# Projections with a queue for each half of the array, 28 more staged groups of maxima, and attention steps of two or three maxima, in a transformer block on one core

## The chip, the core and the metric

One NeuronCore of a Trainium2 chip runs the whole block as one program. The metric is the device time of one execution in microseconds; "time before" is the median of three runs. The engines are TensorE (PE; its weight loads are listed as PEld), VectorE (DVE), ScalarE (ACT), GpSimd (POOL) and SyncE (SP), which here only issues DMAs. TensorE writes to PSUM, which has eight banks of 512 float32 columns on each of 128 partitions.

## The reference

All inputs are float32: x is 2048 x 640, wqkv 640 x 1920, wo 640 x 640, w_gate and w_up 640 x 1728, w_down 1728 x 640. There are 32 heads of 20.

```
q, k, v = split_heads(layernorm(x) @ wqkv)          # 32 heads of 20
p = softmax(q @ k.T * 20 ** -0.5)                   # exact, over 2048 keys
h = x + merge_heads(p @ v) @ wo
out = h + (silu(layernorm(h) @ w_gate) * (layernorm(h) @ w_up)) @ w_down
```

## The kernel before

The program has three stages: the projections to q, k and v, the attention, and the output projection with the feed-forward part. Matmuls whose precision matters are done as three products of values split into a high part and a low part.

**Units and groups.** The 32 heads lie in 8 groups g of 4, and the 2,048 queries in 4 chunks c of 512, which makes 32 attention units u = 4g + c. A head has 20 rows; two heads with the two parts of each make stacks of 60 rows, so that one stack lies in the upper half of the array's rows (partitions 0 to 63, b = 0) and another in the lower half (64 to 127, b = 1). Matmuls in different halves run side by side.

**Maxima.** The softmax needs the largest score of every query before its unit starts. For a unit u, a chunk kc of keys, a tile t of 128 queries and two pairs of heads in both halves there are four products of 128 x 512 scores. They are taken in one of two ways. In attention, `max_one` (products at L274, maxima at L280) does one product of 512 columns into a PSUM bank (`ps_max`, 3 banks there) and one VectorE maximum over it, so that such a set costs four products and four maxima. In the projections, `max_four` does a *staged group*: with keys stored as differences between the two halves of a chunk, four products of 256 columns write a - b to two banks, ScalarE takes the ReLU of each (L251), four products add b (all eight at L239), since max(a, b) = relu(a - b) + b, and VectorE takes a maximum over each bank (L261). `in_projections` says which sets are staged: all of u = 0, and for units with c = 0 or 1 (and u = 2) key chunks 0 and 1. That is 144 groups. The other 1,472 products wait in the lists `singles[0]` and `singles[1]`, one for each half, in the order of the units.

**Projections.** Token chunks c = 0 to 3 are projected one after another: ten blocks of 128 rows of q and k (`query_key`, 512 columns a product) and eight blocks of values (`value`, 320 columns a product), each as 15 products in `rounds` (L643). A product over 128 rows is cut into two of 64 rows. Both halves of a block add to the same PSUM bank, so the second halves must come after the first: `behind` holds them, `second_half` issues one when 20 are waiting, and an instruction on VectorE that does nothing (L648) tells TensorE that the first halves are done. Three banks take blocks, five take maxima. After each product `visit` looks whether something else may be issued: a staged group's second products, a step of the layer norm of the next chunk, a `flip` (transposes of normalised tokens, L569), or a new group. It decides by a planner's clock per engine (`clock`, `takes`) with a duration for each kind of instruction; `held` says when banks come free. Blocks go out through ScalarE copies, GpSimd subtractions (L90) and DMAs to DRAM (L615); staged groups load keys and queries back from DRAM in *items* (L176 on SP's queue), up to six at a time. The order that comes out is fixed in the program.

**Attention.** A unit has 16 steps kt of 128 keys; there are 512 steps. A step follows a string such as `"WsSmmSsM"`: s and S are a score product of 128 x 512 in the upper or lower half (L1303, bank `ps_one`, four in turn) with its exponential on ScalarE (L1309), m and M a maximum from `singles[0]` or `singles[1]`, and W weighs the values of the step two back (L1313; four products, listed as eight). Two strings alternate, with two m and one M or the other way. When the lists are empty, steps have no maximum. Weights of the later stage are prepared on GpSimd meanwhile. The copy of a finished unit is at L1323.

Of the kernel before, what the change touches and what calls it, by code (L numbers as in the profile page):

```python
# [14 lines left out]
ALU = mybir.AluOpType  # L15
# [25 lines left out]
ORDER = ("WsSmmSsM", "WSsMMsSm")  # L41


@with_exitstack
def tile_block(ctx: ExitStack, tc: tile.TileContext, x, wqkv, wo, wg, wu, wd, out):
# [168 lines left out]
    def max_pair(mx, q, k, pair, t, kc, k0):  # L214

        banks = [ps_max() for _ in range(2)]
        for b, ps in enumerate(banks):
            rows = slice(b * ROW, b * ROW + NPART)
            nc.tensor.matmul(
                ps, q[rows, pair, t * P : (t + 1) * P], k[rows, pair, k0 : k0 + CH],  # L220
                start=True, stop=True,
            )
        done = takes("PE", 240)
        for b, ps in enumerate(banks):
            nc.vector.tensor_reduce(
                mx[:, b, pair, t, kc : kc + 1], ps, axis=AX.X, op=ALU.max
            )
            hold([takes("DVE", 600, done + 205) + 100])

    def max_four(mx, q, k, t, kc):  # L230

        banks = [ps_max() for _ in range(2)]
        half = CH // 2

        def products(cols, first):
            for pair in range(2):
                for b in range(2):
                    rows = slice(b * ROW, b * ROW + NPART)
                    nc.tensor.matmul(  # L239
                        banks[b][:, pair * half : (pair + 1) * half],  # L240
                        q[rows, pair, t * P : (t + 1) * P], k[rows, pair, cols],
                        start=first and pair == 0, stop=True, skip_group_check=True,
                    )

        until = [[1e9] for _ in banks]

        def differences():
            products(slice(half, CH), True)
            done = takes("PE", 240)
            for ps in banks:  # L250
                nc.scalar.activation(ps, ps, AF.Relu)  # L251
                takes("ACT", 478, done + 150)
            hold(*until)
            return clock["ACT"] + RELU

        def maxima():
            products(slice(0, half), False)
            done = takes("PE", 240)
            for b, ps in enumerate(banks):
# [3 lines left out]
                    axis=AX.X, op=ALU.max,  # L263
                )

        return differences, maxima

    def max_one(u, kc, t, pair, b):

# [1755 lines left out]
```

## Time and profile before

| | |
|---|---|
| median of 3 runs | 2015.58 us (2015.23 to 2016.2) |
| the profiled execution | 2017.19 us, of which its span 2015.4 |
| first projection product in halves (L643) | 20.9 us after the span's start |
| first score (L1303), last score | 317.9, 1452.7 us |
| busy in the span | PE 2002.7, PEld 1247.8, DVE 1603.9, ACT 1437.1, POOL 796.8 us |
| granted TensorE clock | 1.00 |

A line of a group in the profile reads: source line, engine, operation, output <- input with partitions x elements, count | busy us, mean ns of one | idle time of the engine before, and who ended it. A line of the timeline reads: start, duration, engine, source line, operation, count. A line of a table by stage gives, after the length of the stage, each engine's busy time and the number of its instructions. TensorE's matmuls are pipelined: each is listed with about 0.4 us, but the next of the same half starts 0.12 to 0.23 us later, so starts are compared and not durations.

### The profile page before, as it was taken

To read this page: it belongs to the slowest core of one execution; us is meant where nothing else is said; L and a number is where in the kernel's file an instruction comes from. 1 tells how busy PE (TensorE), PEld (TensorE's weight loads), DVE (VectorE), ACT (ScalarE), POOL (GpSimd) and SP (SyncE) were. 2 spreads that over 40 slices of the span, in tenths; PEclk is the share of its full clock that TensorE was granted. 3 is DMA by queue.
4 is the path that set the end of the run, shared out by engine and by line. 5 is a ranking of instruction groups with operands and counts; after the bars stand their busy time and mean duration, and the time that the engine had idled before them with its cause. 6 is when DMAs were issued, how large, how long until landed. Compare 5 with 4: busy or idle time off the path is not lost.

```text
span 2015.4 us, 40030 instructions
## 1 busy us (share of the span) xinstructions
PE 2002.7 (99%) x14354; PEld 1247.8 (62%) x14354; DVE 1603.9 (80%) x2806; ACT 1437.1 (71%) x2819; POOL 796.8 (40%) x1190
## 2 busy tenths in 40 slices
PE   9999999999999999999999999999999999999999
PEld 8999995333333333333333333345598888888888
DVE  5677778888888888888888988886387666676677
ACT  4678878999999999999999999986633222212221
POOL 7465423333443443343400011011156444754555
PEclk9999999999999999999999999999999999999999
DMA  7777563352634544535513022321159654974642
GB/s 252 255 251 264 179 204 86 117 150 92 190 104 135 159 128 133 160 122 164 172 40 88 22 75 71 94 63 56 40 185 312 223 187 154 354 274 156 206 150 94
DMA packets 199340, 310.35 MB, mean 154 GB/s; under 512 B 53744, under 2 KB 87856, under 8 KB 198120
## 3 DMA queue, kind: packets, MB, share of 16 engines
q1 hardware_dynamic: 192552, 284.21, 43.8%
q0 software_dynamic: 6496, 23.60, 3.9%
q8 instruction: 114, 1.87, 0.4%
q14 instruction: 82, 0.67, 0.1%
q10 hardware_dynamic: 96, 0.00, 0.0%
HBM read 208.11 MB, written 99.19 MB: 152 GB/s over the span
## 4 chain that ended last, share of the span: by engine, by line
PE 96%; DMA 1%; DVE 1%; POOL 1%; issue 0%; ACT 0%; SPq 0%; POOLq 0%; DVEq 0%; ACTq 0%
PE acc L1313 24%; PE ps_a L1481 17%; PE ps_one L1303 15%; PE ps_max L274 12%; PE ps_one L643 10%; PE ps_b L1576 9%; PE ps_max L239 3%; PE ps_max L1031 2%; PE ps_b L1031 2%; PE ps_two L805 0%; PE ps_two L696 0%; DVE mx L261 0%; DMA rb<-r_d 0%; DVE mx L280 0%; PE ps_max L1066 0%
## 5 line engine op out<-in xcount | busy, mean ns | idle before, releaser
L1309 ACT ACTIVATE probs<-ps_one 128x512 f32<-128x512 f32 x2048 | 1056.1, 612 | 61.9 <-PE ps_one L1303 35.0
L280 DVE TENSOR_REDUCE mx<-ps_max 128x1 f32<-128x512 f32 x1472 | 924.5, 683 | 107.0 <-PE ps_one L1303 73.2
L1303 PE MATMUL ps_one<-q_stk,k_stk 62*128 62x512 f32 x2048 | 580.6, 449 | 1.0 <-DMA q_stk<-m_d 1.0
L1313 PE MATMUL acc<-probs,v_stk 128*32 128x512 f32 x4096 | 546.3, 605 | 0.1
L1303 PEld LDWEIGHTS ps_one<-q_stk,k_stk 62*128 62x128 f32 x2048 | 248.0, 184 | 436.6 <-ACT probs L1309 413.9
L274 PE MATMUL ps_max<-k_stk,q_stk 60*128 60x512 f32 x1472 | 374.9, 426 | 1.1 <-DVE mx L261 0.9
L274 PEld LDWEIGHTS ps_max<-k_stk,q_stk 60*128 60x128 f32 x1472 | 272.5, 186 | 29.7 <-DVE mx L280 2.8
L1698 DVE TENSOR_TENSOR tmp<-ps_a,tmp 128x512 f32<-128x512 f32 x208 | 141.2, 689 | 121.0 <-PE ps_a L1481 94.0
L261 DVE TENSOR_REDUCE mx<-ps_max 128x2 f32<-128x512 f32 x288 | 180.6, 684 | 63.8 <-PE ps_max L239 60.2
L1313 PEld LDWEIGHTS acc<-probs,v_stk 128*32 128x32 f32 x4096 | 80.9, 108 | 179.8 <-issue 167.9
L251 ACT ACTIVATE ps_max<-ps_max 128x512 f32<-128x512 f32 x288 | 151.6, 583 | 42.8 <-PE ps_max L239 40.2
L1576 PE MATMUL ps_b<-halves,yp 128*128 128x320 f32 x1032 | 178.7, 308 | 0.2 <-DVE h L1581 0.2
L1576 PEld LDWEIGHTS ps_b<-halves,yp 128*128 128x128 f32 x1032 | 165.2, 188 | 16.0 <-DVE h L1581 0.5
L1481 PE MATMUL ps_a<-t,units 128*128 128x512 f32 x624 | 162.5, 396 | 0.0
L90 POOL TENSOR_TENSOR yp<-y,yp 128x256 fp32r<-128x256 f32 x96 | 60.4, 630 | 186.9 <-ACT yp L89 186.9
L1481 PE MATMUL ps_a<-z,units 128*128 128x512 f32 x516 | 133.9, 394 | 0.0
L1481 PEld LDWEIGHTS ps_a<-t,units 128*128 128x128 f32 x624 | 112.6, 188 | 18.5
L1348 POOL TENSOR_TENSOR o<-o,rb 128x512 f32<-128x512 f32 x31 | 39.9, 1286 | 199.8 <-DMA q_stk<-m_d 72.7
L1581 DVE TENSOR_TENSOR h<-ps_b,h 128x320 f32<-128x320 f32 x248 | 109.7, 480 | 5.8 <-PE ps_b L1576 4.3
L643 PE MATMUL ps_one<-z_hi,w_lo 64*128 64x512 f32 x380 | 113.3, 392 | 0.0
L643 PE MATMUL ps_one<-z_lo,w_hi 64*128 64x512 f32 x380 | 112.1, 392 | 0.0
L643 PE MATMUL ps_one<-z_hi,w_hi 64*128 64x512 f32 x380 | 111.5, 393 | 0.0
(224 smaller groups left out, 2651.7 us busy)
## 6 DMA issues: line engine op xcount, KB each, us to landing
units<-w_d SPq DMA_DIRECT2D x186, 256.0 KB
w_d<-stage SPq DMA_DIRECT2D x106, 256.0 KB
halves<-j_d SPq DMA_DIRECT2D x70, 320.0 KB
j_d<-stage SPq DMA_DIRECT2D x42, 320.0 KB
k_stk<-k_d SPq DMA_DIRECT2D x64, 160.0 KB
q_stk<-q_d SPq DMA_DIRECT2D x64, 160.0 KB
raw<-k_d SPq DMA_DIRECT2D x62, 160.0 KB
raw<-q_d SPq DMA_DIRECT2D x54, 160.0 KB
```

The lines of the kernel that those rows point to most:

```text
L251: nc.scalar.activation(ps, ps, AF.Relu)
L261: nc.vector.tensor_reduce(mx[:, b, :, t, kc], ps.rearrange("p (j n) -> p j n", j=2), axis=AX.X, op=ALU.max,)
L274: nc.tensor.matmul(ps, queries[u][rows, pair, t * P : (t + 1) * P], keys[u // NC][rows, pair, kc * CH : (kc + 1) * CH], start=True, stop=True,
L280: nc.vector.tensor_reduce(mxs[u][:, b, pair, t, kc : kc + 1], ps, axis=AX.X, op=ALU.max)
L643: nc.tensor.matmul(ps, a[rows], b[rows], start=(i == n == 0), stop=(i == 1 and n == last), skip_group_check=True,)
L1303: nc.tensor.matmul(ps, keys[u // NC][rows, p, kt * P : (kt + 1) * P], queries[u][rows, p, :], start=True, stop=True,)
L1309: nc.scalar.activation(probs[p][:, b, :], ps, AF.Exp, scale=scale)
L1313: nc.tensor.matmul(acc[32 * j : 32 * j + 32, :], values[u // NC][:, kt, j * VW : j * VW + 32], probs[j // 2][:, j % 2, :], start=(kt == 0) ...
L1481: nc.tensor.matmul(ps.rearrange("p (t n) -> p t n", t=TPC), w[k][:, i], z[k][:, :, j], start=(first and m == 0), stop=(last and m == len(n ...
L1576: nc.tensor.matmul(ps, a, b, start=(n == 0), stop=(n == len(pairs) - 1))
L1581: nc.vector.tensor_tensor(out=h, in0=ps, in1=h, op=ALU.add)
L1698: add = lambda out, ps, x: nc.vector.tensor_tensor(out=out, in0=ps, in1=x, op=ALU.add)
```

## The change

It has four parts.

1. *A queue for each half.* The planner keeps a time for each half of the array (`lane`), and `other_work` fills whichever is behind. `max_half` takes the place of `max_four`: a staged group becomes two half groups, each with one bank, whose four products are issued one at a time. Second halves of blocks are issued when the planner's time for their first halves has passed, with no fixed lag of 20. The instruction that tells of this (L691 now) goes to VectorE, ScalarE or GpSimd, whichever clock is least, and is issued later, when the first halves should be done. A new half group also waits until VectorE's clock is at most 1,200 ns ahead. A `flip` waits until the layer norm's steps are done.
2. *28 more staged groups*: key chunk 2 of the units u = 4, 8, ... 28. Differences of chunk 2 of the keys are therefore stored for all blocks, and 14 more items are loaded. 172 groups are staged in all, and 1,360 products are left for attention.
3. *Attention:* from step 48 on every fourth step (kt = 3, 7, 11, 15) follows `"WsSmMsS"`, with two maxima.
4. *The end of the maxima of unit 0* uses VectorE's transpose and DMAs (`max_parts`, `max_turn`, `max_load`, as other units do) in the place of a transpose on TensorE (`max_finish`).

```diff
+SHORT = "WsSmMsS"
+FULL_STEPS = 3 * NT
...
-    def max_four(mx, q, k, t, kc):
+    def max_half(mx, q, k, t, kc, b):
+        half, until, own = CH // 2, [1e9], []
+        rows = slice(b * ROW, b * ROW + NPART)
+        def product(pair, cols, first):
             nc.tensor.matmul(
+                own[0][:, pair * half : (pair + 1) * half],
+                q[rows, pair, t * P : (t + 1) * P], k[rows, pair, cols],
+                start=first and pair == 0, stop=True, skip_group_check=True,
             )
+            return spend(b, 118)
+        def difference(pair):
+            if pair == 0:
+                own.append(ps_max())
+                hold(until)
+            done = product(pair, slice(half, CH), True)
+            if pair == 1:
+                nc.scalar.activation(own[0], own[0], AF.Relu)
+                return takes("ACT", 478, done + 150) + RELU
+        def maximum(pair):
+            done = product(pair, slice(0, half), False)
+            if pair == 1:
+                until[0] = takes("DVE", 600, done + 205) + 100
                 nc.vector.tensor_reduce(
+                    mx[:, b, :, t, kc], own[0].rearrange("p (j n) -> p j n", j=2),
                     axis=AX.X, op=ALU.max,
                 )
...
-        return u == 0 or (kc < 2 and (u % NC < 2 or u == 2))
+        return u == 0 or kc < 2 and (u % NC < 2 or u == 2) or kc == 2 and u % NC == 0
...
+    def maxima(b, new=True):
+        if pending[b]:
+            pending[b].pop(0)()
+            return True
+        pe = max(clock["PE"], lane[b])
+        if seconds[b] and seconds[b][0][0] <= pe + SLACK:
+            f = seconds[b].pop(0)[1]
+            f(0)
+            pending[b].append(lambda: f(1))
+            return True
+        if not new or held[0][0] > pe + SLACK or clock["ACT"] > pe + GATE or clock["DVE"] > pe + GATE_DVE:
+            return False
...
+    def other_work(until=None):
+        while True:
+            visit()
+            if lane[1] < lane[0]:
+                if not (maxima(1) or second_half()):
+                    lane[1] = min(lane[0], max(lane[1], clock["PE"]) + 60)
+            elif not maxima(0):
+                if until is None or (until and until[0] <= lane[0] + 50):
+                    return
+                if not (lane[1] <= lane[0] and (maxima(1) or second_half())):
+                    lane[0] += 60
...
-                    if (i, n) == (0, last):
-                        nc.vector.clobber_nop([nc.vector.lower_ap(ps)])
-                        crossed[0] = takes("DVE", 60, clock["PE"] + 450) + 50
+                def cross():
+                    name = min(("DVE", "ACT", "POOL"), key=clock.get)
+                    engine = {"DVE": nc.vector, "ACT": nc.scalar, "POOL": nc.gpsimd}[name]
+                    engine.clobber_nop([engine.lower_ap(ps)])
+                    crossed[0] = takes(name, 60, clock["PE"]) + 50
...
                 half(0)
-                behind.append((half, crossed, done if n == last else None))
-                if len(behind) > LAG:
-                    second_half()
-                visit()
+                spend(0, ns)
+                if n == last:
+                    nops.append((lane[0] + 200, cross))
+                behind.append((half, crossed, done if n == last else None, ns))
...
-            wide = which and (c < 2 or m == 0)
+            wide = which and (c < 3 or m == 0)
...
-            order = ORDER[now[0] % 2] if singles[0] or singles[1] else "WsSsS"
+            if not (singles[0] or singles[1]):
+                order = "WsSsS"
+            elif now[0] >= FULL_STEPS and kt % 4 == 3:
+                order = SHORT
+            else:
+                order = ORDER[full_steps % 2]
+                full_steps += 1
```

What this does to TensorE's queue is seen at two places. The first is the end of the projections: the last blocks of queries (before L643, now L683) and the last staged products (before L239, now L229), up to the first score (L1303, now L1354). Before:

```order
2370 L643 MATMUL ps_one<-z_hi,w_hi 128x512
2371 L239 MATMUL ps_max<-raw 128x256 x4
2372 L643 MATMUL ps_one<-z_hi,w_hi 128x512 x3
2373 L643 MATMUL ps_one<-z_lo,w_hi 128x512 x3
2374 L239 MATMUL ps_max<-raw 128x256 x4
2375 L643 MATMUL ps_one<-z_lo,w_hi 128x512
2376 L239 MATMUL ps_max<-raw 128x256 x4
2377 L643 MATMUL ps_one<-z_lo,w_hi 128x512
2378 L643 MATMUL ps_one<-z_hi,w_lo 128x512 x5
2379 L239 MATMUL ps_max<-raw 128x256 x4
2380 L1303 MATMUL ps_one<-q_stk,k_stk_125 128x512 x2
```

Now, first where the last staged products stand:

```order
2448 L229 MATMUL ps_max<-raw_156,raw_157 128x256 x2
2449 L683 MATMUL ps_one<-z_hi,w_hi 128x512
2450 L683 MATMUL ps_one<-z_hi,w_lo 128x512
2451 L229 MATMUL ps_max<-raw_156,raw_157 128x256
2452 L683 MATMUL ps_one<-z_hi,w_lo 128x512
2453 L229 MATMUL ps_max<-raw_156,raw_157 128x256
```

and the end of it, with the first score in the last row:

```order
2477 L683 MATMUL ps_one<-z_lo,w_hi 128x512
2478 L683 MATMUL ps_one<-z_hi,w_lo 128x512 x6
2479 L683 MATMUL ps_one<-z_hi,w_hi 128x512 x5
2480 L683 MATMUL ps_one<-z_lo,w_hi 128x512 x5
2481 L683 MATMUL ps_one<-z_hi,w_lo 128x512 x5
2482 L1354 MATMUL ps_one<-q_stk,k_stk_125 128x512 x2
```

Staged products came in fours, two for each half; now they come by ones and twos between the blocks' products, and the last of them stand ahead of the last block's second halves, 15 of which (rows 2479 to 2481) end the stage by themselves.

The second place is attention around step 51, one of the steps with kt = 3. Before (W is L1313, scores L1303, maxima L274):

```order
2631 L1313 MATMUL acc<-probs,v_stk_126 32x512 x4
2632 L1303 MATMUL ps_one<-q_stk,k_stk_125 128x512 x2
2633 L274 MATMUL ps_max<-k_stk_5631,q_stk 128x512 x2
2634 L1303 MATMUL ps_one<-q_stk,k_stk_125 128x512 x2
2635 L274 MATMUL ps_max<-k_stk_5631,q_stk 128x512
2636 L1313 MATMUL acc<-probs,v_stk_126 32x512 x4
```

Now (W is L1364, scores L1354, maxima L262):

```order
2738 L1364 MATMUL acc<-probs,v_stk_126 32x512 x4
2739 L1354 MATMUL ps_one<-q_stk,k_stk_125 128x512 x2
2740 L262 MATMUL ps_max<-k_stk_6092,q_stk 128x512 x2
2741 L1354 MATMUL ps_one<-q_stk,k_stk_125 128x512 x2
2742 L1364 MATMUL acc<-probs,v_stk_126 32x512 x4
```

One maximum between the last scores and W is gone in this step; the steps around it stand as before.

More of the change, by code (lines that the diff above doesn't have):

```diff
@@ L219, in max_pair @@
             nc.tensor.matmul(
-                ps, q[rows, pair, t * P : (t + 1) * P], k[rows, pair, k0 : k0 + CH],
-                start=True, stop=True,
-            )
[L223 to L228, printed above, removed]
-    def max_four(mx, q, k, t, kc):
[L232 to L259, printed above, removed]
-                until[b][0] = takes("DVE", 600, done + 205) + 100
@@ L945, in tile_block @@
         store(queue=nc.sync)
[L946 to L948 removed]
+        while finishing:
+            finish_first()
+        assert 0 not in ends
     turn[0], last = 0, jobs[0]
```

142 lines of the change are left out of this document (85 added, 57 removed).

## The prediction

> **What bounds the kernel now.** I read first the chain of work that ended last, then the busy time by stage, then the timeline of TensorE inside two of the stages.
>
> ```profile
> PE 96%; DMA 1%; DVE 1%; POOL 1%; issue 0%; ACT 0%; SPq 0%; POOLq 0%; DVEq 0%; ACTq 0%
> ```
>
> ```profile
> core 0: us, PE busy (x) PEld busy (x) DVE busy (x) ACT busy (x) POOL busy (x), PEclk, DMA share, GB/s
> 20.00:318.00 298.00, 294.44 (x3382) 278.20 (x3383) 215.10 (x362) 220.16 (x427) 154.61 (x213) 1.00 0.72 229
> 318.00:1455.00 1137.00, 1134.80 (x7906) 464.07 (x7902) 976.42 (x1644) 1074.73 (x2105) 333.86 (x548) 1.00 0.35 107
> 1455.00:2015.40 560.40, 555.71 (x2941) 488.21 (x2938) 396.94 (x761) 132.60 (x275) 299.62 (x411) 1.00 0.61 207
> ```
>
> The stages are projections (20 to 318), attention (318 to 1455) and the rest. TensorE has work in flight nearly always: it is idle 298.00 - 294.44 = 3.6 us in projections and 2.2 us in attention. The granted clock is 1.00 throughout. So TensorE's queue sets the time of both stages that the change touches, and the change moves work from one to the other. What counts is how long a staged group holds TensorE and how much a dropped maximum frees. The instructions after attention stand in the same order on every engine before and after, so the third stage counts as unchanged.
>
> **Attention: what a dropped maximum frees.** The timeline of TensorE, first two steps with three maxima, then the one step of this run that has two (the list of maxima ran out in it):
>
> ```profile
> 1000.79 1.07 PE L1313 MATMUL acc<-probs,v_stk 128*32 128x512 f32 x8
> ...
> 1002.92 1.06 PE L1313 MATMUL acc<-probs,v_stk 128*32 128x512 f32 x8
> ...
> 1005.04 1.06 PE L1313 MATMUL acc<-probs,v_stk 128*32 128x512 f32 x8
> ```
>
> ```profile
> 1388.11 1.06 PE L1313 MATMUL acc<-probs,v_stk 128*32 128x512 f32 x8
> 1389.11 0.50 PE L1303 MATMUL ps_one<-q_stk,k_stk 62*128 62x512 f32 x2
> 1389.44 0.40 PE L274 MATMUL ps_max<-k_stk,q_stk 60*128 60x512 f32 x1
> 1389.44 0.39 PE L1303 MATMUL ps_one<-q_stk,k_stk 62*128 62x512 f32 x1
> 1389.67 0.46 PE L274 MATMUL ps_max<-k_stk,q_stk 60*128 60x512 f32 x1
> 1389.68 0.44 PE L1303 MATMUL ps_one<-q_stk,k_stk 62*128 62x512 f32 x1
> 1390.06 1.06 PE L1313 MATMUL acc<-probs,v_stk 128*32 128x512 f32 x8
> ```
>
> From one weighing (L1313) to the next it is 1002.92 - 1000.79 = 2.13 and 1005.04 - 1002.92 = 2.12 us with three maxima, and 1390.06 - 1388.11 = 1.95 us with two. A score or a maximum uses one half of the array's rows; with three maxima the longer half has four in a row, with two each half has three. So a short step saves 2.125 - 1.95 = 0.175 us.
>
> How many there are follows from the code. Before, 1,472 maxima at three a step fill 490 steps and leave two. After, 112 fewer are left, 1,360: 48 steps of three, then three steps of three and one of two in turn, which makes 380 x 3 + 110 x 2 = 1,360, used up in step 489 where it was step 490. Saving: 110 x 0.175 = 19.3 us. The lists of maxima become full as early as before or earlier against the scores that need them.
>
> What could be late next is ScalarE, with four exponentials a step:
>
> ```profile
> 1008.50 0.63 ACT L1323 ACTIVATE o<-acc 128x512 f32<-128x512 f32 x1
> 1008.98 4.07 ACT L1309 ACTIVATE probs<-ps_one 128x512 f32<-128x512 f32 x8
> ```
>
> It starts one 128x512 activation 1008.98 - 1008.50 = 0.48 us after another, so four take 1.92 us, under 1.95. The second row gives an upper end: (4.07 - 0.63)/7 = 0.49 each, 1.97 us a step. I take the two-maxima step as it was measured and keep 1.97 for a rival. VectorE gets a quarter of a maximum per step less to do, so no wait arises there.
>
> **Projections: what 28 more groups cost.** The costs per instruction, from the page's groups:
>
> ```profile
> L280 DVE TENSOR_REDUCE mx<-ps_max 128x1 f32<-128x512 f32 x1472 | 924.5, 683 | 107.0 <-PE ps_one L1303 73.2
> L261 DVE TENSOR_REDUCE mx<-ps_max 128x2 f32<-128x512 f32 x288 | 180.6, 684 | 63.8 <-PE ps_max L239 60.2
> L251 ACT ACTIVATE ps_max<-ps_max 128x512 f32<-128x512 f32 x288 | 151.6, 583 | 42.8 <-PE ps_max L239 40.2
> ```
>
> A staged group is eight 256-column products, two ReLUs and two maxima over 512 columns; 28 more make 224 products (L239 goes from 1,152 to 1,376 in the program), 56 ReLUs and 56 maxima. VectorE gets 56 x 180.6/288 = 35.1 us, ScalarE 56 x 151.6/288 = 29.5 us. In 298 us they were busy 215.1 and 220.2; with 311 us to do it in, they come to about 250 us each, 80%. So they need not become the bound, but have less room when a product waits for a bank. The timeline of TensorE around two half groups shows what the products cost:
>
> ```profile
> 180.41 0.39 PE L643 MATMUL ps_one<-z_hi,w_lo 64*128 64x512 f32 x1
> ...
> 180.64 0.39 PE L643 MATMUL ps_one<-z_hi,w_lo 64*128 64x512 f32 x1
> ...
> 181.11 0.48 PE L239 MATMUL ps_max<-raw,raw 60*128 60x256 f32 x4
> 181.35 0.40 PE L643 MATMUL ps_one<-z_hi,w_lo 64*128 64x512 f32 x1
> 181.43 0.40 PE L643 MATMUL ps_one<-z_lo,w_hi 64*128 64x512 f32 x1
> 181.58 0.48 PE L239 MATMUL ps_max<-raw,raw 60*128 60x256 f32 x4
> 181.83 0.40 PE L643 MATMUL ps_one<-z_hi,w_lo 64*128 64x512 f32 x1
> ```
>
> A 512-column product holds its half for 180.64 - 180.41 = 0.23 us. Four products of a group, two in each half, delay the projections by 181.35 - 181.11 = 0.24 and 181.83 - 181.58 = 0.25 us, so a group costs 0.48 us and 28 cost 13.4 us. They lie on the path, since TensorE has only 3.6 us idle here.
>
> [...] Each product has a weight load of its own:
>
> ```profile
> L239 PEld LDWEIGHTS ps_max<-raw,raw x608: 182/186/192, 66.7 to 303.3; 60*128 60x128 f32 x152
> ```
>
> [...]
>
> **The two queues** change when products go, not how many. What they could save: the idle 3.6 us, whose waits are few,
>
> ```profile
> PE ps_max L569 <- DVE xt L551: 1.8, 2, 1.0
> PE ps_max L239 <- ACT ps_max L251: 0.9, 2, 0.6
> PE ps_max L239 <- DVE mx L261: 0.4, 1, 0.4
> ```
>
> the 0.01 to 0.02 us by which a pass of four is longer than 0.23 (288 passes, some 4.3 us), and stretches with work in one half only. Before, the second halves ran 20 products late, so 20 x 0.23 = 4.6 us at the end are work of one half; the rows of order at the end of the projections now show 15 products left (3.5 us), a gain of 1.1. Together at most 9.0 us. What they could cost: a group's ReLU now gets two products per half with other work between, and 70 small waits that tell the second halves that the first are done go to whichever of three engines the planner holds to be free, where all were on VectorE. A product that waits holds both halves, since the queue of TensorE is one. I bound the cost by two thirds of the 70 (the code spreads them; 23 each), each half an instruction of its engine late:
>
> ```profile
> L90 POOL TENSOR_TENSOR e<-e 128x512 fp32r<-128x512 f32 x14 | 18.0, 1289 | 47.7 <-ACT e L89 47.7
> ```
>
> 23 x 1.289/2 = 14.8 on GpSimd and 23 x 0.583/2 = 6.7 us on ScalarE, 21.5 us if nothing hides it. The planner keeps clocks for these engines, and the second halves of most rounds have other work ahead of them. Between -9.0 and +21.5 I take 0, since the old waits (3.6 us) are the nearest row and lie near it.
>
> Edits with one answer: four more wide copies in chunk 2 (VectorE, ScalarE and GpSimd, each off the path at 80% or less) and 56 more loads on SP's queue (14 items; the DMA share is 0.72 here, mostly late in the stage where it falls) cost nothing while the loads are planned ahead; a load that lands late would hold both halves. The end of the first unit's maxima goes through DMA, some 200 products ahead of the first score, instead of a transpose on TensorE: nothing.
>
> **The sum.** -19.3 + 13.4 + 0 = -5.9 us. The profiled execution took 2017.19 us (its span of 2015.4 and 1.8 around it); the median of the runs is 2015.58, and I set the difference against that: 2009.7 us. About 0.2%, 4.0 us, is what a measurement of this kernel can tell from no change.
>
> **Rivals.** (a) *The forecast*, 2009.7, from 2006 to 2014 as the waits go by -4 to +4 us: chance 0.55, of which 0.36 below 2011.5 and 0.19 within 0.2%. For it: both terms are measured steps of this trace.
>
> (b) *The small waits hold TensorE* (slower): a wait for the first halves stands behind an instruction on GpSimd or ScalarE, the second half's product waits, and both halves with it. Half of the 21.5 us gives 10.8: 2020.5. It decides from 5.9 us, 27% of the price. For it: GpSimd's rows of 1.29 us and engines at 80%; against it: rounds of which the second half follows late. Chance 0.16.
>
> (c) *The queues pay*: all 9.0 us come back, 2000.7. For it: stretches with one half; against it: TensorE idles only 3.6 us. Chance 0.15.
>
> (d) *ScalarE takes over the short steps*: 1.97 us instead of 1.95 leaves 110 x 0.155 = 17.1 us, 2011.9; if it also loses its lead after the copy at L1323, a little more. Chance 0.08, within 0.2%.
>
> (e) *Evacuation becomes the bound of the projections*: each added group shows its two maxima, 28 x 2 x 0.627 = 35.1 us, less the 13.4 it hides: 2009.7 + 21.7 = 2031.4. Against it: VectorE at 72% before. Chance 0.05. [...]
>
> (f) *Weight loads that don't overlap*: with products alternating between the halves, each load of 0.186 us comes on top of 0.12 us, 28 x 4 x 0.306 = 34.3 instead of 13.4: 2030.6. Two products of a half in 0.24 us speak against it. Chance 0.01.
>
> **How the numbers follow.** The predicted time is (a)'s, 2009.7. The range leaves out (e) and (f), the upper part of (b) and the lower edge of (c): 2001 to 2021. Faster: 0.36 + 0.15 = 0.51. Within 0.2%: 0.19 + 0.08 = 0.27. Slower: 0.16 + 0.05 + 0.01 = 0.22.
>
> **What would show it.** Right: weighings 1.95 us apart in every fourth step of attention and 2.12 in the others, attention about 19 us shorter; the first score at 318 + 13 = 331 us; TensorE idle in projections by about 4 us. Wrong: a first score after 337 (b, e; the waits of TensorE then name L691's engine or VectorE), or before 325 (c); short steps over 2.0 us with ScalarE as releaser (d); any change of the time from the end of attention to the end, which I count at none.

## The result and the profile after

The changed kernel takes 2030.89 us in the median of four runs (2029.3 to 2036.58) against 2015.58: a ratio of 1.0081, with an interval of 1.0061 to 1.0100. It is slower by 0.8%, and above the range of the prediction. Its profiled execution, the fastest of the four, took 2029.3 us, 12.1 more than the 2017.19 of the one before; the medians are 15.3 apart, and what follows accounts for the 12.1.

Where the 12.1 us are is read first from the three stages, cut at the first score and after the last. The row that heads them is that of the scores (L1354), whose last part gives when the first and the last of them start:

```profile
L1354 PE MATMUL ps_one<-q_stk,k_stk x2048: 383/492/522, 350.0 to 1464.7; 62*128 62x512 f32 x187
```

```profile
core 0: us, PE busy (x) PEld busy (x) DVE busy (x) ACT busy (x) POOL busy (x), PEclk, DMA share, GB/s
20.00:350.00 330.00, 319.06 (x3602) 295.29 (x3601) 249.94 (x424) 250.82 (x482) 156.63 (x213) 0.99 0.73 231
350.00:1467.00 1117.00, 1116.19 (x7796) 467.32 (x7794) 910.45 (x1530) 1063.67 (x2105) 334.18 (x550) 1.00 0.36 109
1467.00:2027.50 560.50, 555.45 (x2941) 488.15 (x2938) 395.91 (x761) 132.56 (x275) 298.65 (x411) 1.00 0.60 207
```

The first score comes at 350.0 us where it came at 317.9: the projections are 32.1 us longer. From first to last score it is 1114.7 where it was 1134.8: attention is 20.1 us shorter. From the last score to the end of the span it is 562.8 and was 562.7. So 32.1 - 20.1 + 0.1 = 12.1. In the projections TensorE is idle for 330.00 - 319.06 = 10.9 us, where it had been 3.6, and the granted clock is no longer 1.00.

Attention looks as forecast. Weighings (L1364) follow each other on TensorE's timeline so:

```profile
1003.22 1.07 PE L1364 MATMUL acc<-probs,v_stk 128*32 128x512 f32 x8
1005.35 1.06 PE L1364 MATMUL acc<-probs,v_stk 128*32 128x512 f32 x8
1007.30 1.06 PE L1364 MATMUL acc<-probs,v_stk 128*32 128x512 f32 x8
1009.43 1.06 PE L1364 MATMUL acc<-probs,v_stk 128*32 128x512 f32 x8
```

A short step takes 1007.30 - 1005.35 = 1.95 us, those beside it 2.13.

The waits of TensorE in the projections (20 to 350 us; total, times, longest) are other ones than before:

```profile
PE ps_max L229 <- DMA raw<-k_d: 5.4, 1, 5.4
PE ps_max L229 <- ACT ps_max L242: 3.0, 5, 1.3
PE ps_max L229 <- DMA raw<-q_d: 1.9, 2, 1.0
PE ps_max L619 <- DVE mx L249: 0.3, 1, 0.3
PE ps_one L683 <- DVE e L92: 0.2, 1, 0.2
```

and those of its weight loads, which stand in the same queue (partly the same waits, seen one instruction earlier):

```profile
PEld ps_max L229 <- ACT ps_max L242: 6.0, 14, 1.5
PEld ps_max L229 <- DVE mx L249: 3.0, 8, 1.3
...
PEld ps_one L683 <- ACTq L691: 0.4, 1, 0.4
```

Before, no product waited for a load. Now the longest wait is one, and the instructions that tell of the first halves (L691) hold hardly anything, 0.4 us. The timeline of TensorE around the longest wait:

```profile
171.96 0.28 PE L229 MATMUL ps_max<-raw,raw 60*128 60x256 f32 x1
...
172.08 0.28 PE L229 MATMUL ps_max<-raw,raw 60*128 60x256 f32 x1
...
173.13 0.39 PE L229 MATMUL ps_max<-raw,raw 60*128 60x256 f32 x2
178.94 0.55 PE L229 MATMUL ps_max<-raw 60*128 60x256 f32 x1 [5.42 <-DMA raw<-k_d]
...
179.50 0.41 PE L229 MATMUL ps_max<-raw,raw 60*128 60x256 f32 x1
...
179.72 0.41 PE L229 MATMUL ps_max<-raw,raw 60*128 60x256 f32 x1
```

Blocks' products (L683) stand behind the waiting one, and both halves of the array are idle. After it, products of 256 columns in a row start 179.72 - 179.50 = 0.22 us apart, where it had been 172.08 - 171.96 = 0.12: the granted clock is 0.50. The table by 20 us has it:

```profile
140.00:160.00 20.00, 20.00 (x294) 19.76 (x293) 15.95 (x27) 18.47 (x38) 9.94 (x11) 1.00 0.70 222
160.00:180.00 20.00, 14.58 (x180) 14.04 (x177) 13.27 (x21) 12.99 (x27) 2.21 (x4) 0.91 0.72 231
180.00:200.00 20.00, 18.70 (x180) 17.51 (x180) 16.95 (x34) 13.22 (x25) 8.11 (x8) 0.92 0.69 208
```

A mean of 0.91 over 20 us is 3.6 us at half clock, the 0.92 after it 3.2: together 6.8 us, from 176.4 to 183.2. TensorE had work again from 178.94, so some 4.3 us of it were worked at half speed, which costs 2.1. SP's timeline shows when the loads of that group were issued:

```profile
167.79 2.33 SPq L365 DMA_DIRECT2D xt<-in_A_x  x4
170.34 8.06 SPq L178 DMA_DIRECT2D raw<-q_d  x8
```

The first product that reads the first of these items was due at 178.94 - 5.42 = 173.5, some 3 us after that item's first issue at 170.3. The planner counts 8 us, so the issue came some 5 us later than planned. From issue to product it was 178.94 - 170.34 = 8.6 us, about what the planner counts.

### The profile page after: what moved, and what is told of

It is laid out like the page before. It is cut to its first block, busy times and chain, and to the rows that moved or that the text cites. A ratio compares the mean times of both kernels' runs of the same rounds, so it can differ in the third digit from the quotient of the medians.

```text
span 2027.5 us, 40445 instructions
## 1 busy us (share of the span) xinstructions
PE 2008.4 (99%) x14465; PEld 1268.1 (63%) x14465; DVE 1571.8 (78%) x2754; ACT 1456.7 (72%) x2874; POOL 797.9 (39%) x1192
## 3 DMA queue, kind: packets, MB, share of 16 engines
q8 instruction: 115, 1.88, 0.4%
## 4 chain that ended last, share of the span: by engine, by line
PE 88%; DMA 1%; DVE 0%; ACT 0%; issue 0%; SPq 0%; POOL 0%; POOLq 0%; ACTq 0%; DVEq 0%
PE acc L1364 25%; PE ps_a L1538 17%; PE ps_one L1354 16%; PE ps_max L262 11%; PE ps_b L1633 9%; PE ps_one L683 4%; PE ps_max L229 2%; PE ps_max L1082 2%; PE ps_b L1082 2%; DMA raw<-q_d 0%; PE ps_max L1117 0%; DMA v_d<-ev 0%; PE ps_a L1904 0%; SPq L178 0%; DVE mx L249 0%
## 5 line engine op out<-in xcount | busy, mean ns | idle before, releaser
L268 DVE TENSOR_REDUCE mx<-ps_max 128x1 f32<-128x512 f32 x1360 | 857.7, 684 | 151.3 <-PE ps_one L1354 75.5
L1354 PE MATMUL ps_one<-q_stk,k_stk 62*128 62x512 f32 x2048 | 561.4, 451 | 0.5 <-ACT probs L1360 0.5
L1364 PE MATMUL acc<-probs,v_stk 128*32 128x512 f32 x4096 | 546.3, 605 | 0.1
L1354 PEld LDWEIGHTS ps_one<-q_stk,k_stk 62*128 62x128 f32 x2048 | 261.7, 184 | 450.6 <-ACT probs L1360 430.6
L262 PE MATMUL ps_max<-k_stk,q_stk 60*128 60x512 f32 x1360 | 346.6, 420 | 0.1
L249 DVE TENSOR_REDUCE mx<-ps_max 128x2 f32<-128x512 f32 x344 | 216.4, 684 | 53.8 <-PE ps_max L229 48.7
L262 PEld LDWEIGHTS ps_max<-k_stk,q_stk 60*128 60x128 f32 x1360 | 231.5, 186 | 15.5 <-DVE mx L268 0.4
L242 ACT ACTIVATE ps_max<-ps_max 128x512 f32<-128x512 f32 x344 | 183.2, 584 | 34.4 <-PE ps_max L229 29.4
L1364 PEld LDWEIGHTS acc<-probs,v_stk 128*32 128x32 f32 x4096 | 80.9, 108 | 155.8 <-issue 143.6
L229 PE MATMUL ps_max<-raw 60*128 60x256 f32 x672 | 104.0, 293 | 8.4 <-DMA raw<-k_d 5.4
L229 PE MATMUL ps_max<-raw,raw 60*128 60x256 f32 x704 | 107.7, 291 | 2.0 <-ACT ps_max L242 1.0
L1538 PEld LDWEIGHTS ps_a<-z,units 128*128 128x128 f32 x516 | 93.1, 187 | 16.0
```

The costliest lines, as they stand in the source:

```text
L229: nc.tensor.matmul(own[0][:, pair * half : (pair + 1) * half], q[rows, pair, t * P : (t + 1) * P], k[rows, pair, cols], start=first and pa ...
L242: nc.scalar.activation(own[0], own[0], AF.Relu)
L249: nc.vector.tensor_reduce(mx[:, b, :, t, kc], own[0].rearrange("p (j n) -> p j n", j=2), axis=AX.X, op=ALU.max,)
L262: nc.tensor.matmul(ps, queries[u][rows, pair, t * P : (t + 1) * P], keys[u // NC][rows, pair, kc * CH : (kc + 1) * CH], start=True, stop=True,
L268: nc.vector.tensor_reduce(mxs[u][:, b, pair, t, kc : kc + 1], ps, axis=AX.X, op=ALU.max)
L1354: nc.tensor.matmul(ps, keys[u // NC][rows, p, kt * P : (kt + 1) * P], queries[u][rows, p, :], start=True, stop=True,)
```

## The experiments

The comparisons are with the kernel before on the same chip and in the same job, where it took 2015.6 us in the median for the first row and 2016.8 to 2017.8 for the others. "First score" is that of each kernel's one profiled run. Runs of one kernel lie 1 to 15 us apart, so a difference of one or two microseconds between first scores says little. Kernel 1 is the kernel of experiment 1, and so on.

| kernel | time, us | ratio to before (95%) | first score, us |
|---|---|---|---|
| changed kernel | 2030.89 | 1.0081 (1.0061 to 1.0100) | 350.0 |
| the two queues alone | 2028.97 | 1.0054 (1.0037 to 1.0072) | 329.4 |
| - and no later loads | 2017.73 | 1.0002 (0.9992 to 1.0011) | 319.8 |
| - and 10 us for a load | 2023.33 | 1.0029 (1.0017 to 1.0040) | 324.7 |
| changed, no later loads | 2022.95 | 1.0024 (1.0013 to 1.0035) | 340.3 |
| changed, wider margins | 2023.20 | 1.0042 (1.0024 to 1.0059) | 338.5 |
| short steps alone | 1999.35 | 0.9912 (0.9898 to 0.9925) | 318.4 |

**1. The two queues alone.** Edit on the changed kernel:

```diff
-        return u == 0 or kc < 2 and (u % NC < 2 or u == 2) or kc == 2 and u % NC == 0
+        return u == 0 or kc < 2 and (u % NC < 2 or u == 2)
-FULL_STEPS = 3 * NT
+FULL_STEPS = NT * 10000
```

and the lists of added groups and the wide chunk 2 as before.

> Only the queue for each half: the 144 staged groups of before, three maxima in every step, chunk 2 of the keys stored as before. Theory A (the 28 groups' loads come late and TensorE stands, then runs at half clock): with 14 items fewer the loads keep up, so 2012 to 2020 us, first score at 314 to 322. Theory B (the two queues cost by themselves, through small waits for ReLUs, maxima and first halves that hold both halves): some 10 to 19 us slower than before, 2026 to 2035, first score at 328 to 337.

Measured: 2028.97 us, first score at 329.4. The queues alone cost 11.5 us of projections, with no product more in them, and the waits name loads again:

```profile
PE ps_max L229 <- DMA raw<-q_d: 4.6, 5, 3.0
```

**2. The old queue with the 28 groups.** The kernel before with the groups and the short steps, and the planner's gates opened so that the groups fit; `SLACK` lets a product go 600 ns ahead of what it waits for.

```diff
-        LANDING, LANDING_FIRST, SLACK, GATE, APART = 8000, 14000, 0, 500, 2500
+        LANDING, LANDING_FIRST, SLACK, GATE, APART = 8000, 14000, 600, 2000, 2000
```

> Only the 28 groups and the steps with two maxima, on the old queue; its gates are loosened (a group may start while banks are 600 ns and ScalarE 2,000 ns behind, items may load 2,000 ns apart), since with the old gates 28 groups were left over at the end of the projections. Theory A: the loads are as many, so waits for them remain: first score at 331 plus 3 to 12 us, 2013 to 2023 us in all. Theory B: the groups cost their 13.4 us and little more, first score near 331, 2008 to 2012 us.

Measured: 2097.24 us, ratio 1.0387 (1.0366 to 1.0408), first score at 416.8. Its weight loads waited for ReLUs:

```profile
PEld ps_max L241 <- ACT ps_max L253: 41.5, 131, 2.9
```

With the gates opened the old queue issues second products before their ReLUs are done. So this shows what such waits cost, and not what 28 groups cost in that queue, which stays open.

**3. The small instructions on VectorE alone** (rival b).

```diff
-                    name = min(("DVE", "ACT", "POOL"), key=clock.get)
+                    name = "DVE"
```

> The changed kernel with all of the small waits for first halves on VectorE, as before the change. Theory A: no change beyond 3 us from the changed kernel's 2031. Theory B, in the form of the prediction's rival (GpSimd and ScalarE hold the waits up): 5 us or more faster, under 2026.

Measured: 2027.89 us, ratio 1.0045 (1.0029 to 1.0061), first score at 349.7 against 350.0. The projections of the profiled run are as long, and a load was waited for again, at another place (3.0 us before 295.8). So where the instructions go is not the main cause. That it costs nothing is not shown: this profile is of the slowest of five runs, the changed kernel's of the fastest of four, and the medians are 3.0 us apart.

**4. No later loads.** The first six items are loaded; the later ones read the same tiles, so the maxima are those of other rows. TensorE's queue is that of the changed kernel.

```diff
-                if n % 6 >= 4:
+                if n >= 6:
+                    t = kept[n % 6]
+                elif n % 6 >= 4:
...
-                stack(t, which, g, c, slice(CH // 2, EW) if which else slice(0, CH))
+                if n < 6:
+                    kept.append(t)
+                    stack(t, which, g, c, slice(CH // 2, EW) if which else slice(0, CH))
```

> The changed kernel without the loads of items 7 to 72: the staged products read the first six items again, so the maxima are those of other keys and queries; the order on TensorE is the same. Theory A: the waits for loads (7.3 us in the profile) and the stretch at half clock (6.8 us, worth about 3.4) go: 9 to 13 us faster than the changed kernel, 2018 to 2022, first score at 337 to 341. Theory B: 3 us or less faster, 2028 to 2031.

Measured: 2022.95 us, first score at 340.3, 9.7 us earlier. No load is waited for, and the clock stays whole:

```profile
20.00:340.00 320.00, 315.19 (x3601) 292.13 (x3600) 249.64 (x424) 250.76 (x482) 156.36 (x213) 1.00 0.46 136
```

The 9.7 us are about the 5.4 + 1.9 us of waits for loads and the 2.1 of half clock. 22.4 us of longer projections are left, though.

**5. The two queues alone, no later loads.** Edit 4 on kernel 1.

> The two queues alone (144 groups and always three maxima, as before), with only the first six items loaded; all later items read the tiles of those six, so the maxima are those of other rows. TensorE's queue is that of the run with the queues alone, which took 2029.0 us. Theory A, loads that land late are most of what the queues cost: about 2018 us, within 2 us of the kernel before, first score at 318 to 320 us. Theory B, the finer mix of staged products among the blocks' products costs by itself (waits for ReLUs and maxima, and what stands behind them): 2022 to 2026 us, first score at 323 to 327 us with no wait for a load.

Measured: 2017.73 us, the time of the kernel before; first score at 319.8:

```profile
L1358 PE MATMUL ps_one<-q_stk,k_stk x2048: 384/492/522, 319.8 to 1451.5; 62*128 62x512 f32 x187
```

Theory A holds: of the 11.5 us, loads cost 9.6 and the two queues themselves 1.9. The rows of kernel 1 name 4.6 of the 9.6 as waits for loads, and some 3.2 us at half clock (0.98 and 0.94 in the mean of the 20 us to 180 and to 200) cost 1.6 more; its weight loads also wait longer for maxima (4.5 us, 1.1 here). It also gives the price of the groups without loads: 340.3 - 319.8 = 20.5 us, not 13.4. The waits for ReLUs and maxima of this kernel, and after them those of kernel 4:

```profile
PE ps_max L229 <- ACT ps_max L242: 1.5, 3, 0.9
...
PE ps_max L229 <- DVE mx L249: 0.2, 1, 0.2
...
PEld ps_max L229 <- ACT ps_max L242: 4.2, 12, 1.3
...
PEld ps_max L229 <- DVE mx L249: 1.1, 3, 0.5
```

```profile
PE ps_max L229 <- ACT ps_max L242: 3.0, 5, 1.3
PE ps_max L229 <- DVE mx L249: 1.2, 2, 1.0
...
PEld ps_max L229 <- ACT ps_max L242: 6.1, 14, 1.5
PEld ps_max L229 <- DVE mx L249: 2.7, 6, 1.2
```

On the products they come to 1.7 us here and 4.2 there, on the weight loads to 5.3 and 8.8. These are partly the same waits, so they can't be added up.

**6. Both halves' staged products side by side.** Kernel 4, with the lower half made to take a staged product whenever the upper does (`one` is the old `maxima`).

```diff
         def maxima(b, new=True):
+            if b:
+                return False
+            if not one(0, new):
+                return False
+            SLACK_NOW[0] = 1e6
+            assert one(1, new)
+            SLACK_NOW[0] = SLACK
+            return True
```

> The changed kernel without the loads of items 7 and on (2023.0 us in its first run, first score at 340.3 us), and with one more edit: when the upper half takes a staged product, the lower half takes its own right after it, so that both halves' staged products stand side by side as before. Same number of products, ReLUs and maxima. Theory B, the mix of a staged product in one half with a block's product in the other costs TensorE's time: 2015 to 2019 us, first score at 332 to 336 us. Theory C, the mix costs nothing and the rest are waits for ReLUs and maxima: 2021 to 2026 us, first score at 338 to 343 us, with the waits for L242's ReLUs as many or more.

Measured: 2100.71 us, ratio 1.0419 (1.0405 to 1.0433), first score at 419.0:

```profile
PEld ps_max L229 <- ACT ps_max L242: 90.1, 175, 1.5
```

A bad experiment for its question: the lower half was made to go when the upper half's ReLU was done, and its own comes after that on ScalarE. It does give a price: 175 weight loads waited 0.51 us each, and the first score came 78.7 us later than that of kernel 4. Waits that short, repeated, held both halves: from 20 to 340 us TensorE was idle for 320 - 285.46 = 34.5 us, where it was 4.8 in kernel 4.

**7. Wider margins, all the work kept.**

```diff
-    RELU = 150
+    RELU = 300
-        LANDING, LANDING_FIRST, SLACK, GATE, APART = 8000, 14000, 0, 500, 2500
+        LANDING, LANDING_FIRST, SLACK, GATE, APART = 10000, 14000, 0, 500, 2500
-                    name = min(("DVE", "ACT", "POOL"), key=clock.get)
+                    name = "DVE"
```

> The changed kernel, all its work, with three margins of the planner widened: 10 us instead of 8 us from a load's issue to its landing, 300 ns instead of 150 ns after a ReLU, and the small instructions that tell of the first halves always on VectorE. Theory A (late loads, and the half clock after them, are 8 to 10 us of the loss, ReLUs some 2 to 3): 2018 to 2022 us, no wait of over 1 us for a load and a granted clock of 1.00. If the loads' lateness is only moved elsewhere (the queue of SP is the limit): 2028 to 2032 us, with such waits at other places.

Measured: 2023.20 us in the median, from 2018.87 to 2033.55, so wide that one run in six lay where the changed kernel does. In the profiled run, the fastest, the clock is whole and one load is waited for:

```profile
PE ps_max L229 <- DMA raw<-q_d: 0.3, 1, 0.3
```

The median gains about as much as leaving the loads out, and stays 0.42% slower than before.

**8. The short steps alone.** The kernel before with `SHORT` as in the change; the 112 maxima are left out.

```diff
-        if not in_projections(u, kc, t)
+        if not in_projections(u, kc, t) and not (kc == 2 and u % NC == 0)
```

> The kernel before with the short steps alone: the 112 maxima over key chunk 2 of the units 4, 8, ... 28 are left out altogether (their places are filled with -1e30 once), so the projections stay as before. If a short step saves 0.175 us: 110 x 0.175 = 19.3 us less than the kernel before, a ratio of 0.9904, first score at 318 us. Rival, the gain in attention depends on where the projections end or on the queues: a ratio over 0.993.

Measured: 1999.35 us, 17.4 less (ratio 0.9912, 0.9898 to 0.9925). The 19.3 lies inside the interval; the profile has 1115.8 us from first to last score, 19.0 less:

```profile
L1307 PE MATMUL ps_one<-q_stk,k_stk x2048: 383/492/522, 318.4 to 1434.2; 62*128 62x512 f32 x187
```

**9. A longer margin after ReLUs, no later loads.** Kernel 4 and one number:

```diff
-    RELU = 150
+    RELU = 450
```

> The changed kernel without the loads of items 7 and on (their products read the first six items' tiles), and the planner counts 450 ns instead of 150 ns from a ReLU's planned end to the second products that need it. Without the margin this kernel's first score came at 340.3 us, its time was 2023.0 us; the two queues alone without loads had 319.8 us, so 28 groups took 20.5 us there where 13.4 were forecast. Theory D, the missing 7 us are products that wait for ReLUs and maxima: the waits for L242 fall below half (3.0 us of TensorE, 6.1 us of its weight loads before), first score at 334 to 337 us, 2017 to 2020 us. Theory B, the products cost more among the blocks' products even without waits: waits fall and the first score stays at 339 to 342 us, 2021 to 2024 us.

Measured: 2022.39 us, ratio 1.0022 (1.0013 to 1.0032), first score at 342.3. Inconclusive: fewer weight loads wait for ReLUs (4 where it was 14), but the order has changed, and products wait for GpSimd's part of the next chunk's tokens, after which products of 512 columns of one half start 89.11 - 88.68 = 0.43 us apart, where it had been 0.24 (the mean clock is 0.99 from 20 to 335 us):

```profile
PE ps_one L689 <- POOL z_hi L642: 3.7, 2, 1.9
PE ps_max L229 <- ACT ps_max L242: 2.2, 2, 1.4
...
PEld ps_max L229 <- DVE mx L249: 3.7, 14, 0.9
PEld ps_max L229 <- ACT ps_max L242: 3.3, 4, 1.8
```

**10. The x loads on another queue.** The changed kernel and one line of `load_x`:

```diff
-                nc.sync.dma_start(xs[t], x[t * P : (t + 1) * P, :])
+                (nc.scalar if c else nc.sync).dma_start(xs[t], x[t * P : (t + 1) * P, :])
```

> The changed kernel with all its loads and the same order on TensorE; only the loads of x for chunks 1 to 3 are issued on ScalarE's queue instead of SP's. In the changed kernel the longest wait for a load, 5.4 us at 173.5, was for an item issued behind x loads of chunk 2. If those x loads are what made it late: no such wait, a granted clock of 1.00 through the projections, first score at 341 to 345 us instead of 350.0, 2022 to 2026 us. If SP's queue is slow by itself or memory is busy: 2029 to 2033 us with a wait of several us at this or another place. If ScalarE's queue is held by the issue of the loads: more waits for L242.

Measured: 2029.80 us, ratio 1.0060 (1.0043 to 1.0076), first score at 348.5. The row of waits for loads is now:

```profile
PE ps_max L229 <- DMA raw<-q_d: 4.7, 4, 2.7
```

Its longest wait stands before the same product as that of the changed kernel and that of kernel 1, the 541st staged one, and is 2.7 us where it was 5.4:

```profile
171.20 4.30 SPq L178 DMA_DIRECT2D raw<-q_d  x8
176.63 0.35 PE L229 MATMUL ps_max<-raw 60*128 60x256 f32 x1 [2.66 <-DMA raw<-q_d]
```

The item was issued no earlier (171.2 us here, 170.3 there), but its product went 5.4 us after the issue and not 8.6. So the x loads look like a part of what made it late, and not all of it. Nor are they out of the way. SP's issues around this place wait for x loads to land, for 3.9 us in the changed kernel, and here for

```profile
SPq L178 <- DMA xt<-in_A_x: 4.4, 4, 1.9
```

**11. Margins, and x loads and v stores on ScalarE's queue.** Kernel 7 with edit 10 and

```diff
-                nc.sync.dma_start(v_d[rows], ev)
+                nc.scalar.dma_start(v_d[rows], ev)
```

> The changed kernel with all its work, the wider margins of the earlier run (10 us for a load, 300 ns for a ReLU, small instructions on VectorE), and the loads of x for chunks 1 to 3 and the stores of v on ScalarE's queue. With margins alone the runs went from 2018.9 to 2033.6 us, 2023.2 in the median. If what is left of that spread are loads held behind others on SP's queue: 2017 to 2020 us with a spread of under 5 us, as fast as the kernel before within 0.2% and not faster. If ScalarE is held by them: over 2023 us.

Measured: 2038.71 us, ratio 1.0100 (1.0081 to 1.0120), first score at 358.4. ReLUs are waited for longer than in kernel 7, where these rows have 2.3 and 4.6 us, which fits the last line, that the issues hold ScalarE:

```profile
PE ps_max L229 <- ACT ps_max L242: 7.9, 10, 2.2
...
PEld ps_max L229 <- ACT ps_max L242: 14.2, 23, 2.4
```

A load was waited for as well, for 3.1 us, and the mean granted clock of the profiled run is 0.995, where the other profiled runs have 0.997 to 1.000.

**12 and 13. The bare pair.** Kernels 4 and 5 without the ReLUs and maxima of the staged groups, so that no product waits for them. TensorE's queue is the same as with them.

```diff
-                nc.scalar.activation(own[0], own[0], AF.Relu)
...
-                nc.vector.tensor_reduce(
-                    mx[:, b, :, t, kc], own[0].rearrange("p (j n) -> p j n", j=2),
-                    axis=AX.X, op=ALU.max,
-                )
```

> The changed kernel without the loads of items 7 and on, and without the ReLUs and maxima of all staged groups (maxima set to 0 once): every product stands in TensorE's queue where it stood, but none waits for a ReLU, a maximum or a load. With ReLUs and maxima: 2023.0 us, first score at 340.3 us. Theory D, the 7 us by which 28 groups cost more than 13.4 are waits for ReLUs and maxima: first score at 328 to 333 us, and 13 to 15 us after that of the same kernel without the 28 groups. Theory B, the order of single products costs TensorE by itself: 335 to 340 us, and 18 to 21 us after it.

> The same bare kernel without the 28 groups and with three maxima in every step of attention (the two queues alone, no loads of items 7 and on, no ReLUs and maxima of staged groups). With ReLUs and maxima: 2017.7 us, first score at 319.8 us. Theory D: first score at 314 to 317 us, 3 to 6 us earlier. Theory B: within 2 us of 319.8, since few waits for ReLUs are there (1.5 us of TensorE, 4.2 of its weight loads).

Measured: 2004.98 us and first score at 321.9 with the 28 groups; 2009.52 us and 313.3 without.

```profile
L1357 PE MATMUL ps_one<-q_stk,k_stk x2048: 383/492/759, 321.9 to 1440.2; 62*128 62x512 f32 x187
```

The queue of the changed kernel, then, runs 18.4 us faster (340.3 - 321.9) when nothing has to be waited for: the order of single products costs little, and theory B falls. The edit also takes most of the work of VectorE and ScalarE out of the stage (39 and 76 us busy, 250 and 251 with it), so what it prices is the ReLUs and maxima with all that fuller engines delay. Without the 28 groups 6.5 us are gained. That kernel lost some of it again, since its products came so soon that one of the first six loads was late:

```profile
PE ps_max L231 <- DMA raw<-q_d: 3.4, 2, 2.5
```

```profile
60.00:80.00 20.00, 16.56 (x230) 16.14 (x228) 2.86 (x4) 4.03 (x9) 4.93 (x7) 0.91 0.42 144
```

Those are 3.4 us and 3.6 us at half clock, 5.2 together, so that without them it would be 308.1. The 28 groups' products cost 321.9 - 313.3 = 8.6 to 13.8 us, and the ReLUs and maxima that came with them 18.4 - 6.5 = 11.9 down to 20.5 - 13.8 = 6.7 us. Neither figure met its expectation; what they tell apart they do.

**14. The two queues alone with 10 us for a load.** Kernel 1 and

```diff
-        LANDING, LANDING_FIRST, SLACK, GATE, APART = 8000, 14000, 0, 500, 2500
+        LANDING, LANDING_FIRST, SLACK, GATE, APART = 10000, 14000, 0, 500, 2500
```

> The two queues alone with all their loads (2029.0 us in the first run, first score at 329.4 us), with one number of the planner changed: 10 us instead of 8 us from a load's issue to its landing. Theory A, products are placed before their loads land: 2016 to 2021 us, first score at 318 to 322 us, no wait for a load over 1 us. If wider margins only shift the waits: 2025 us and more.

Measured: 2023.33 us, first score at 324.7. Between the two: 4.7 of the 9.6 us are back, and three waits for loads of 0.5 to 0.8 us are left, but more weight loads wait for maxima (5.6 us, 10 times; 4.5 and 8 in kernel 1).

```profile
PE ps_max L229 <- DMA raw<-k_d: 1.2, 2, 0.7
PE ps_max L229 <- DMA raw<-q_d: 0.8, 1, 0.8
...
PEld ps_max L229 <- DVE mx L249: 5.6, 10, 1.0
```

## Why the prediction was wrong

**Attention, -19.3.** Right: -20.1 in the profile, -19.0 with the short steps alone, 1.95 us a short step. Rival (d) did not come: ScalarE kept up.

**The products of 28 groups, 13.4.** It lies inside what the bare pair gives as the price of the products, 8.6 to 13.8, with 13.8 the end corrected for that pair's own late load. Rival (f), weight loads that don't overlap, gave 34.3, and falls.

**The steps that failed** are two. The first is "56 more loads on SP's queue ... cost nothing while the loads are planned ahead; a load that lands late would hold both halves". The condition was named and then neither priced nor made a rival. It was not the 56 more loads, either: the two queues without them lose 9.6 us in the same way, the changed kernel 9.7. The planner places a product as soon as its 8 us have passed by its own clock, and at the 5.4 us wait SP had come to the loads some 5 us later than planned. The time from the last load of an item to the first product that reads it follows from the traces and the order of the items in each program. In the kernel before it was 7.2 us or more, and 13.5 in the middle. With the two queues 3 of 52 items (those after the first six) had under 6 us, and the middle was 11.5; in the changed kernel 5 of 66, and 11.7; with wider margins 1 of 66, and 11.9. Not every short one is waited for: four of the five in the changed kernel had 4.8 to 5.9 us and no wait before that product. The fifth is the wait of 5.4 us, whose product was due 0.6 us after its last load. The kernel before had slack that its list of waits does not show. That is the step to learn from: that the idle time is one "whose waits are few" was read from a queue with a lag of 20 products, which the change took away.

The second is "they need not become the bound, but have less room when a product waits for a bank", to which the sum gave nothing. 28 groups took 20.5 us without loads where the sum had 13.4: 7.1 more. They come with ReLUs and maxima, which the bare pair puts at 6.7 to 11.9; the rows of waits for these grow by 2.5 us on the products and 3.5 on the weight loads from kernel 5 to kernel 4. How the 7.1 divide between these waits and other work that came later on fuller engines is not shown.

**The two queues, 0 from -9.0 to +21.5.** By the parts: 1.9 for the queues themselves, 9.7 for loads and the half clock after them, 7.1 for ReLUs and maxima: 18.7, inside the bounds and near their upper end. 13.4 + 18.7 = 32.1, the measured change of the projections, as it must be, since the 7.1 are what the 13.4 leave of the 20.5. That the bounds held is luck: the upper one was made of waits for the small instructions (L691), whose rows have 0.4 us, and priced neither loads nor ReLUs. The value was taken at the nearest row, which belonged to the old queue; the range, cut at 2021, left the upper end out.

**The rivals.** (b) had the right shape, a wait that holds both halves, with the wrong releaser: L691 has 0.4 us, and with all of those instructions on VectorE the profiled run has the first score where it was. The sign named for (b) and (e), a first score after 337 us, came, but the longest wait names a load. (e) comes to a number near the result, 2031.4, by another way: VectorE and ScalarE are busy for 250 of 330 us, and without late loads the time is 2023. (c) did not come; the queues paid nothing back.

**What stays open:** why SP issues items later than planned. With the x loads on ScalarE's queue the late item was issued no earlier, and SP's issues waited as long for x loads to land; what else holds SP there was not taken apart. And no version with the 28 groups beat the kernel before: the best, with wider margins, is 0.42% slower; the two queues alone with 10 us for a load are 0.29% slower. By the prediction's prices a group saves 19.3/28 = 0.69 us in attention and costs 0.48 us of products, so 0.21 us a group, 5.9 in all, was there to win at best.

## What to carry to other kernels

A queue that is closed up loses the slack that hid its loads: ask of every operand how long before its use it is issued, before and after, and price the case in which it is late, with both halves or all that stands behind. A wait that the profile of before does not show is not thereby free; when the change removes a lag, bound it by the margin and not by the old waits. And leaving work out one kind at a time, with the order kept, tells in two runs what the waits of a full engine queue are made of.

## What the runs showed of the hardware

A short idle time of TensorE cost more than itself. In the changed kernel it was idle for 5.42 us up to 178.94, and the granted clock was 0.50 for 6.8 us, from 176.4 to 183.2. In kernels 1, 10 and 13 the longest waits were 2.99, 2.66 and 2.47 us (the last with one of 0.97 us 2 us later); the mean clocks of the stretches of 20 us there, 0.98 and 0.94, 0.97 and 0.95, and 0.91, make 3.2, 3.2 and 3.6 us at half clock. After 3.02 and 0.87 us close together (kernel 3) products of 320 columns of one half started 0.27 us apart, where it had been 0.15. The longest wait alone does not tell the cases apart: with waits of up to 1.3 us the clock stayed at 1.00 in the projections of kernels 4 and 5, but in kernel 6, after waits of 1.18 and 0.35 us that ended at 232.5 and 234.1 us, products of 512 columns of one half started 0.43 us apart, where it had been 0.24; so they did in kernel 9 after 1.82 and 1.88 us that ended 2.9 us apart. What idle time brings the clock down is not shown.

In the bare kernel with single products of the two halves in any order, 3,600 products and their weight loads ran with 298.91 of 301.00 us busy:

```profile
20.00:321.00 301.00, 298.91 (x3600) 287.63 (x3600) 39.08 (x80) 76.45 (x138) 156.26 (x213) 1.00 0.49 144
```

These weight loads are listed with up to 0.19 us each (0.185 to 0.186 in the mean, the transposes' apart) and come to some 660 us together, more than the 2 x 301 us that the two halves have. So by the listed times they run beside products of the same half too.
